# Attention scores from plain f32 matmuls on two halves of the array, in place of split operands

## The chip, the cores and the metric

The kernel runs on one core of a Trainium2 chip. The metric is the device time in microseconds (us) of one execution; where several runs are shown, their median. The profile is one execution recorded by the hardware profiler.

## The reference, cut to what matters

```python
# q, k, v: (4, 8, 1152, 64)    w_in: (512, 2048)    w_out: (2048, 512), all f32
q_pool = q.reshape(B, H, S // 2, 2, D).mean(axis=3)             # 576 queries a head
scores = (1 / sqrt(D)) * q_pool @ k^T                           # 576 x 1152 a head
scores = scores - max(scores, axis=-1)
attn   = exp(scores) / (sum(exp(scores)) + 1e-9)
x      = attn @ v                                               # heads joined: 2304 x 512
h      = x @ w_in                                               # 2304 x 2048
out    = (h * clip(h + 3, 0, 6) / 6) @ w_out                    # 2304 x 512
```

## The kernel before

The 32 heads are taken as 16 pairs (`NG`). The 576 queries of a head are cut into 64 and four times 128. A pair thus has nine score tiles of 128 query rows: one that holds the 64 rows of both heads (`j` is None in the code), and four for each head. There are 144 tiles `i` in all. A tile's 1152 keys are taken in three pieces `c` of 384 columns.

**Operands of the scores.** The kernel wants more precision than one f32r matmul gives, so it splits each operand into an upper part (rounded to f32r) and the remainder. For each head, `upper_k` and `lower_k` put both parts of k beside each other (64 + 64 columns); `turn_k` (L333) transposes this on TensorE into 128 rows, `take_k` copies it from PSUM to SBUF (`kT`). `pool_q` writes the sum of neighbouring queries twice beside each other, `turn_q` (L346) transposes it, and `take_q` splits the result into `qh` (ScalarE, L355) and `ql` (VectorE, L357). One piece of scores (`scores`, L384) is then two f32r matmuls with a contraction of 128: `qh` with both parts of k, and `ql` with both parts of k. A None tile takes four, two for each head, with zeros in the rows of the other head.

**What follows a score piece.** `least` (L392, VectorE) copies it out of PSUM with the running minimum of the negated scores; `expo` (ScalarE), `recip` (VectorE) and `normal` (GpSimd) make the softmax; `turn` (L423) transposes it on TensorE in three pieces of three 128x128 transposes, in f32; `take` copies these out; `values` (L448) multiplies with v in plain f32, each head into 64 of the 128 output rows (64 columns of the array). The result is split and spilled to DRAM, two groups of query columns a pair (320 and 256).

**The rest.** The weights of the gated layer are converted to a split form early and stored in DRAM (`w_d`). `layer` (L172) and `project` (L205) read them back, 512 KB at a time, for 6 chunks of 256 tokens times 16 blocks of the hidden dimension. The last 768 tokens are done at the end, when the attention is over.

**Order.** The order of the instructions on every engine and on the DMA queue (all DMAs are issued by SyncE) is written out in advance by `Order.run`, a list planner with a cost for each step and a place in a priority list; the chip then keeps that order on each engine. Tiles below `WIDE` use the first part's PSUM layout: score buffers `v`, two of two banks each, evacuated two pieces at once and then one. At tile `WIDE` the function `second_part` takes these banks away; from then on the scores have two banks `s`, and `layer` and `project` get theirs and run between the attention's steps.

The matmuls of the scores:

```python
            for x in q_t[g % 2]:
                for jj in ((0, 1) if j is None else (j,)):
                    o = 0 if j is None else 2 * REST + t * P
                    ops.append((x[:, jj, o:o + P], kT[g, jj, c]))
            for m, (x, kk) in enumerate(ops):
                nc.tensor.matmul(ps, x, kk.rearrange("p t k -> p (t k)"), start=(m == 0), stop=(m == len(ops) - 1))
```

Of the kernel before, what the change touches and what calls it, by code (L numbers as in the profile page):

```python
# [11 lines left out]
F32 = mybir.dt.float32  # L12
# [12 lines left out]
NEAR = 5  # L25
WIDE = 40
# [87 lines left out]
def pooled_attention_then_gated_mlp(ctx, tc, q, k, v, w_in, w_out, out):  # L114
# [130 lines left out]
    with ExitStack() as a:  # L245
        ld = a.enter_context(tc.tile_pool(name="ld", bufs=2))
        kq = a.enter_context(tc.tile_pool(name="kq", bufs=4 * KT // KC))
        sp = a.enter_context(tc.tile_pool(name="sp", bufs=5))
        sm = a.enter_context(tc.tile_pool(name="sm", bufs=6))
# [9 lines left out]
        for n in range(2):  # L259
            both = []  # L260
            for nm in ("qh", "ql"):
                t = const.tile([P, 2, QW], F32R, name=f"{nm}{n}")
                for j in range(2):
                    z = slice(REST * (1 - j), REST * (2 - j))
                    nc.vector.tensor_copy(out=t[:, j, z], in_=zero.to_broadcast([P, REST]))
                both.append(t)
            q_t.append(both)
# [4 lines left out]
        EARLY = [(0, 0), (0, 1), (None, 0), (1, 0), (1, 1)] + TILES[5:]  # L272
        NTI = len(TILES)
        GROUPS = ((0, REST + 2 * P), (REST + 2 * P, SQ - REST - 2 * P))

        def tiles(g):
            return TILES if g else EARLY

# [8 lines left out]
        def load_k(eng, g, j):  # L287
            b, h = pair(g, j)
            kr_t[g, j] = ld.tile([P, KT, D], F32, tag="kr", name="kr")
            nc.sync.dma_start(out=kr_t[g, j], in_=k[b, h].rearrange("(p t) d -> p t d", p=P))  # L290

        def load_q(eng, g, j):
            b, h = pair(g, j)
            qr_t[g, j] = ld.tile([QP, QT, 2, D], F32, tag="qr", name="qr")
            nc.sync.dma_start(out=qr_t[g, j], in_=q[b, h].rearrange("(p t r) d -> p t r d", p=QP, r=2))
# [14 lines left out]
        def pool_q(eng, g, j, r):  # L310
            if r == 0:
                qp_t[g, j] = ld.tile([QP, QT, 2, D], F32, tag="qp", name="qp")
            x = qr_t[g, j]
            by[eng].tensor_tensor(out=qp_t[g, j][:, :, r, :], in0=x[:, :, 0, :], in1=x[:, :, 1, :], op=ALU.add)

        def upper_k(eng, g, j):
            ks_t[g, j] = ld.tile([P, KT, 2, D], F32R, tag="ks", name="ks", bufs=1)
            copy(eng, ks_t[g, j][:, :, 0, :], kr_t[g, j])

        def lower_k(eng, g, j):  # L320
            ks = ks_t[g, j]
            by[eng].tensor_tensor(
                out=ks[:, :, 1, :], in0=kr_t[g, j], in1=ks[:, :, 0, :].bitcast(F32), op=ALU.subtract
            )
# [4 lines left out]
        def turn_k(eng, g, j, c):  # L329
            ps = tr_t["k", g, j, c] = near(g)[0].tile([P, KC, P], F32R, tag=near(g)[1], name="ptk")  # L330
            for t in range(KC):
                src = ks_t[g, j][:, KC * c + t, :, :].rearrange("p r d -> p (r d)")
                nc.tensor.transpose(ps[:, t, :], src, identr)  # L333

        def take_k(eng, g, j, c):
            kT[g, j, c] = kq.tile([P, KC, P], F32R, tag="kT", name="kT")
            copy(eng, kT[g, j, c], tr_t.pop(("k", g, j, c)))


        QPARTS = (((0, REST, 0), (REST, SQ // 2, 2 * REST)), ((0, SQ // 2, REST + SQ // 2),))  # L340

        def turn_q(eng, g, j, half):
            ps = tr_t["q", g, j, half] = near(g)[0].tile([P, SQ // 2], F32, tag=near(g)[1], name="ptq")
            for t in range(QT // 2):
                src = qp_t[g, j][:, half * (QT // 2) + t, :, :].rearrange("p r d -> p (r d)")
                nc.tensor.transpose(ps[:, t * QP:(t + 1) * QP], src, ident[:QP, :QP])  # L346

        def take_q(eng, g, j, half):
            qh, ql = q_t[g % 2]
            ps = tr_t["q", g, j, half]  # L350
            for c0, c1, to in QPARTS[half]:
                to = to or REST * j
                o = slice(to, to + c1 - c0)
                if eng == "ACT":
                    nc.scalar.copy(out=qh[:, j, o], in_=ps[:, c0:c1])  # L355
                else:
                    nc.vector.tensor_tensor(  # L357
                        out=ql[:, j, o], in0=ps[:, c0:c1], in1=qh[:, j, o].bitcast(F32), op=ALU.subtract
                    )

        def pieces(i):

            return [(0, 2), (2, 3)] if i < WIDE else [(c, c + 1) for c in C3]

        def bank(i):
            return "v" if i < WIDE else "s"

        def scores(eng, i, c):
            g, n = divmod(i, NTI)
            j, t = tiles(g)[n]  # L370
            tag = bank(i)
            if c in [c0 for c0, _ in pieces(i)]:
                pool, n = (ps_m["s"], 1) if tag == "s" else (ps_w, 2)
                ps_t[i] = pool.tile([P, n, DM], F32, tag=tag, name="pqk", bufs=2), c
                ps_t[i, c] = ps_t[i]
            tile, c0 = ps_t[i]
            ps = tile[:, c - c0, 0:NK]
            ops = []
            for x in q_t[g % 2]:
                for jj in ((0, 1) if j is None else (j,)):  # L380
                    o = 0 if j is None else 2 * REST + t * P
                    ops.append((x[:, jj, o:o + P], kT[g, jj, c]))
            for m, (x, kk) in enumerate(ops):
                nc.tensor.matmul(ps, x, kk.rearrange("p t k -> p (t k)"), start=(m == 0), stop=(m == len(ops) - 1))  # L384

        def least(eng, i, c):
            if c == 0:
                s_t[i] = sp.tile([P, S], F32, tag="s", name="s")
                cm_t[i] = sm.tile([P, KC], F32, tag="cm", name="cm")
            s, cm = s_t[i], cm_t[i]  # L390
            end = dict(pieces(i))[c]
            nc.vector.tensor_scalar(  # L392
                out=s[:, c * NK:end * NK].rearrange("p (c k) -> p c k", k=NK), in0=ps_t.pop((i, c))[0][:, 0:end - c, 0:NK],
                scalar1=-SCALE, scalar2=cm[:, c - 1:c] if c else None,
                op0=ALU.mult, op1=ALU.min, accum_out=cm[:, end - 1:end],
            )
# [32 lines left out]
        def take(eng, i, c):  # L429
            g, gr = group(i)  # L430
            j, t = tiles(g)[i % NTI]
# [132 lines left out]
        room = dict(kr=2, qr=2, qp=2, ks=1, vr=2, tr=2, kT=12, tx=1, s=2, S=5, pt0=1, pt1=1, av=1, xo=2,  # L564
# [5 lines left out]
        def halves(j, t):  # L570

            if j is None:
                return [(0, 0), (1, 0)]
            return [(j, n) for n in range(2) if t in ((0, 1), (1, 2, 3))[n]]

        for g in range(NG):
            z0 = 3 * NTI * g
            lead = z0 - 3 * NTI
            early = g == 0
            for j in range(2):  # L580
                add(("lk", g, j), lead - 8 + 9 * j, {"SP": (470, 2500, 900)}, partial(load_k, g=g, j=j), (), ("kr",))
                add(("lq", g, j), lead - 8 + 9 * j + .5, {"SP": (470, 2500, 900)}, partial(load_q, g=g, j=j), (), ("qr",))
                z = lead + 2 + 7 * j
                for r in range(2):
                    cost = {"DVE": (480, 560)} if early else {"POOL": (1100, 1110)}
                    add(("pq", g, j, r), z + 1 + r, cost, partial(pool_q, g=g, j=j, r=r),
                        [("pq", g, j, 0)] if r else [("lq", g, j)], () if r else ("qp",), ("qr",) if r else ())
                cost = {"ACT": (580, 680)} if early else {"POOL": (780, 790), "ACT": (580, 680, 4)}
                add(("uk", g, j), z, cost, partial(upper_k, g=g, j=j), [("lk", g, j)], ("ks",))
                cost = {"DVE": (690, 760)} if early else {"POOL": (1490, 1500)}  # L590
                add(("dk", g, j), z + .5, cost, partial(lower_k, g=g, j=j), [("uk", g, j)], (), ("kr",))
                for c in C3:
                    add(("tk", g, j, c), z + 4 + 2 * c, {"PE": (255, 475)}, partial(turn_k, g=g, j=j, c=c),
                        [("dk", g, j)], (near(g)[1],), ("ks",) if c == 2 else ())
                    add(("ek", g, j, c), z + 4 + 2 * c, MOVE, partial(take_k, g=g, j=j, c=c),
                        [("tk", g, j, c)], ("kT",), (near(g)[1],))
                for n in range(2):
                    add(("tq", g, j, n), z + 5 + 2 * n, {"PE": (255, 475)}, partial(turn_q, g=g, j=j, half=n),
                        [("pq", g, j, 1)], (near(g)[1],), ("qp",) if n else ())
                    needs = [("tq", g, j, n)]  # L600
                    if g > 1:
                        needs += [("mm", NTI * (g - 1) - x, 2) for x in (1, 2)]
# [160 lines left out]
```

## Time and profile before

| what | value |
|---|---|
| median of 3 runs | 989.78 us (989.46 to 992.21) |
| span of the profiled execution | 988.8 us |
| TensorE (PE) busy | 942.5 us, 95% |
| VectorE (DVE) busy | 590.6 us, 60% |
| ScalarE (ACT) busy | 532.6 us, 54% |
| GpSimd (POOL) busy | 362.2 us, 37% |
| DMA | 204 MB, 206 GB/s over the span |

PE busy counts a matmul from its start to its modelled end, and matmuls overlap in the array; so the distance between the starts of two matmuls, and not the duration of one, says what a matmul costs the engine. PEld is the loading of the stationary operand, which overlaps matmuls.

### The profile page before, as it was taken

Reading aid. Unit: us, or ns where it says so; the run is one execution under the profiler, and the core shown is the slowest. Engines: PE = TensorE matmul, PEld = TensorE weight load, DVE = VectorE, ACT = ScalarE, POOL = GpSimd, SP = SyncE. Lnnn points to the kernel's source line nnn. Section 1 sums busy time; section 2 is a strip of 40 time slices with the busy share of each in tenths; the row PEclk is TensorE's granted clock in tenths of the full one; section 3 lists DMA queues with packets and bytes.
Section 4 is the critical chain, followed back from the end, with each engine's and each line's share of the span. In section 5 each row is a group of like instructions: output and inputs, shape, how many; then the busy total and the mean of one; then the engine's idle time right before and its main releaser. Section 6 shows DMA issues by size and latency. Waiting matters only on the chain.

```text
span 988.8 us, 17816 instructions
## 1 busy us (share of the span) xinstructions
PE 942.5 (95%) x6288; PEld 783.6 (79%) x6288; DVE 590.6 (60%) x1752; ACT 532.6 (54%) x1098; POOL 362.2 (37%) x338
## 2 busy tenths in 40 slices
PE   5898997999999999999999999999999999999997
PEld 4676676677678888888888878888898887788886
DVE  5787788678687766566575756566565552222222
ACT  4786786666565656455564555455564542222222
POOL 3876867545565434333251423323121110000000
PEclk9999997999999999999999999999999999999999
DMA  5875565788777476568475766557565668633332
GB/s 174 274 231 192 178 202 174 227 288 287 265 252 240 153 224 199 183 207 285 159 252 163 235 223 217 200 176 276 185 226 168 223 229 283 219 127 126 127 124 85
DMA packets 80888, 204.06 MB, mean 206 GB/s; under 512 B 7840, under 2 KB 31392, under 8 KB 80800
## 3 DMA queue, kind: packets, MB, share of 16 engines
q1 hardware_dynamic: 80800, 202.93, 62.6%
q8 instruction: 50, 0.82, 0.3%
q14 instruction: 38, 0.31, 0.1%
HBM read 171.97 MB, written 30.93 MB: 205 GB/s over the span
## 4 chain that ended last, share of the span: by engine, by line
PE 80%; DVE 9%; DMA 5%; ACT 3%; issue 2%; POOL 1%; SPq 0%; ACTq 0%; DVEq 0%; POOLq 0%
PE ph L172 18%; PE po L205 15%; PE pav L448 14%; PE pqk L384 13%; PE ptp L423 11%; PE pt L205 4%; DVE s L392 3%; DMA w<-w_d 3%; PE ptk L333 2%; PE ptq L346 1%; DVE gl L190 1%; DMA raw<-in_moe_w_in_dram 1%; DMA raw<-in_moe_w_out_dram 1%; ACT s L401 1%; DVE pcv L503 1%
## 5 line engine op out<-in xcount | busy, mean ns | idle before, releaser
L412 POOL TENSOR_SCALAR s<-s,den 128x1152 f32<-128x1152 f32 x144 | 177.8, 1235 | 340.1 <-DVE den L408 204.9
L423 PE MATMUL ptp<-ident,s 128*128 128x128 f32 x1296 | 209.1, 277 | 8.3 <-ACT pt L306 4.8
L401 ACT ACTIVATE s<-s,cm 128x1152 f32<-128x1152 f32 x144 | 181.7, 1262 | 40.7 <-DVE s L392 39.6
L384 PE MATMUL pqk<-kT,qh 128*128 128x384 f32 x480 | 184.9, 402 | 6.3 <-DVE s L392 5.2
L172 PE MATMUL ph<-mxmxh,w 128*128 128x256 f32 x896 | 184.3, 289 | 6.0 <-DMA w<-w_d 4.9
L423 PEld LDWEIGHTS ptp<-ident,s 128*128 128x128 f32 x1296 | 156.6, 142 | 39.2 <-issue 9.6
L306 ACT COPY pt<-ptp 128x384 f32<-128x384 f32 x296 | 138.7, 481 | 77.3 <-PE ptp L423 75.0
L392 DVE TENSOR_SCALAR_CACHE_REDUCE s<-pqk,cm 128x384 f32<-128x384 f32 x248 | 151.0, 609 | 32.0 <-PE pqk L384 27.7
L384 PE MATMUL pqk<-kT,ql 128*128 128x384 f32 x480 | 156.8, 343 | 0.0
L172 PEld LDWEIGHTS ph<-mxmxh,w 128*128 128x128 f32 x896 | 147.1, 191 | 11.5 <-DMA w<-w_d 4.5
L448 PE MATMUL pav<-pt,vr 128*64 128x256 f32 (+1 forms) x1152 | 149.2, 410 | 0.1
L205 PE MATMUL po<-w,gh 128*128 128x512 f32 x448 | 140.6, 395 | 0.0
L177 ACT ACTIVATE r<-ph,three 128x256 f32<-128x256 f32 (+1 forms) x128 | 63.8, 499 | 142.2 <-PE ph L172 141.9
L172 PE MATMUL ph<-mxmxl,w 128*128 128x256 f32 x448 | 126.7, 283 | 0.0
L448 PEld LDWEIGHTS pav<-pt,vr 128*64 128x64 f32 x1152 | 78.9, 137 | 56.7 <-issue 6.2
L181 DVE SCALAR_TENSOR_TENSOR r<-r,ph 128x256 f32<-128x256 f32 (+1 forms) x128 | 57.6, 450 | 97.8 <-ACT r L177 97.2
L308 DVE COPY pt<-ptp 128x384 f32<-128x384 f32 x136 | 74.9, 553 | 56.3 <-PE ptp L423 55.8
L392 DVE TENSOR_SCALAR_CACHE_REDUCE s<-pqk 128x384 f32<-128x384 f32 (+1 forms) x144 | 95.4, 662 | 16.6 <-PE pqk L384 15.0
L384 PEld LDWEIGHTS pqk<-kT,qh 128*128 128x128 f32 x480 | 89.1, 193 | 16.1 <-DVE s L392 11.4
L205 PE MATMUL po<-w,gl 128*128 128x512 f32 x224 | 93.5, 417 | 6.8 <-DVE gl L190 3.5
L205 PEld LDWEIGHTS po<-w,gh 128*128 128x128 f32 x448 | 84.8, 189 | 14.8
L190 DVE TENSOR_TENSOR gl<-r,gh 128x256 fp32r<-128x256 f32 (+1 forms) x128 | 79.1, 618 | 28.7 <-ACT gh L185 28.2
(55 smaller groups left out, 1132.8 us busy)
## 6 DMA issues: line engine op xcount, KB each, us to landing
w<-w_d SPq DMA_DIRECT2D x224, 512.0 KB, 4.6
w_d<-scratch SPq DMA_DIRECT2D x32, 512.0 KB, 3.7
kr<-in_k_dram SPq DMA_DIRECT2D x32, 288.0 KB, 4.6
qr<-in_q_dram SPq DMA_DIRECT2D x32, 288.0 KB, 4.8
vr<-in_v_dram SPq DMA_DIRECT2D x16, 576.0 KB, 5.3
raw<-in_moe_w_in_dram SPq DMA_DIRECT2D x16, 512.0 KB, 4.3
raw<-in_moe_w_out_dram SPq DMA_DIRECT2D x16, 512.0 KB, 4.3
mxmxh<-xh_d SPq DMA_DIRECT2D x7, 512.0 KB, 6.1
```

The costliest lines, as they stand in the source:

```text
L172: nc.tensor.matmul(ps, w[:, wi, cs], x[:, c, :], start=(m == 0), stop=(m == 3 * NCC - 1))
L177: nc.scalar.activation(out=r6, in_=ps, func=AF.Relu, bias=three)
L190: nc.vector.tensor_tensor(out=gl, in0=r6, in1=gh.bitcast(F32), op=ALU.subtract)
L205: nc.tensor.matmul(o, g[:, ts], w[:, wi, :], start=(f == 0 and n == 0), stop=(f == NFC - 1 and n == 2))
L306: nc.scalar.copy(out=out, in_=in_)
L308: by[eng].tensor_copy(out=out, in_=in_)
L384: nc.tensor.matmul(ps, x, kk.rearrange("p t k -> p (t k)"), start=(m == 0), stop=(m == len(ops) - 1))
L392: nc.vector.tensor_scalar(out=s[:, c * NK:end * NK].rearrange("p (c k) -> p c k", k=NK), in0=ps_t.pop((i, c))[0][:, 0:end - c, 0:NK], scal ...
L401: nc.scalar.activation(out=s, in_=s, func=AF.Exp, bias=cm_t.pop(i)[:, KC - 1:], scale=-1.0, accum_out=den_t[i])
L412: nc.gpsimd.tensor_scalar(out=s, in0=s, scalar1=den_t.pop(i), scalar2=1.0, op0=ALU.mult, op1=ALU.mult)
L423: nc.tensor.transpose(ps[:, x, :], s_t[i][:, o:o + P], ident)
L448: nc.tensor.matmul(av[j * D:(j + 1) * D, :], vr_t[g][:, j, t, :], pt_t[g, gr][:, t, j, :], start=(t == 0), stop=(t == KT - 1),)
```

## The change

Scores are computed in plain f32. Neither k nor q is split.

- k of both heads of a pair is loaded in one DMA of 576 KB (before, two of 288 KB), and so is q. `join_k` puts the two heads beside each other (64 + 64 columns), `pool_q` does the same for q; so one transposition serves both heads: per pair 9 of k (f32 in place of 18 in f32r) and 6 of q (in place of 12).
- After it, rows 0 to 63 of `kT` and of q hold head 0 and rows 64 to 127 head 1. One step of `scores` issues two f32 matmuls with a contraction of 64: head 0 on rows 0 to 63 of the array, head 1 on rows 64 to 127, each into a PSUM bank of its own. The None tile is one f32 matmul with a contraction of 128 (the zeros are kept).
- Two tiles (the same rows of both heads) thus get their scores together, and take both `s` banks at once in the second part. `least` evacuates one piece of 384 at a time throughout.
- The pair's first tile needs both heads; the order `EARLY` of the first pair (head 0 first) is gone. `WIDE` is 41. `kT` has 6 buffers in place of 12, `s` in SBUF 7 in place of 5, the raw q one of double size in place of two. Loads of weights (`lw`) must keep their order.

```diff
-            both = []
-            for nm in ("qh", "ql"):
-                t = const.tile([P, 2, QW], F32R, name=f"{nm}{n}")
...
+            t = const.tile([P, QW], F32, name=f"q{n}")
+            nc.vector.tensor_copy(out=t[:, 0:2 * REST], in_=zero.to_broadcast([P, 2 * REST]))
...
+        def join_k(eng, g, j):
+            if j == 0:
+                ks_t[g] = ld.tile([P, KT, 2, D], F32, tag="ks", name="ks", bufs=1)
+            copy(eng, ks_t[g][:, :, j, :], kr_t[g][:, j])
...
-                nc.tensor.transpose(ps[:, t, :], src, identr)
...
+                nc.tensor.transpose(ps[:, t, :], ks_t[g][:, KC * c + t, :, :].rearrange("p j d -> p (j d)"), ident)
...
+        def take_q(eng, g, half):
+            t, ps = q_t[g % 2], tr_t["q", g, half]
+            if half == 0:
+                for j in range(2):
+                    d = slice(j * D, (j + 1) * D)
+                    copy(eng, t[d, j * REST:(j + 1) * REST], ps[d, 0:REST])
+                copy(eng, t[:, 2 * REST:REST + SQ // 2], ps[:, REST:])
+            else:
+                copy(eng, t[:, REST + SQ // 2:], ps)
...
+        def space(i):
+
+            if i < WIDE:
+                t = ps_w.tile([P, 2, DM], F32, tag="v", name="pqk", bufs=2)
+                return [t[:, x, 0:NK] for x in range(2)]
+            return [ps_m["s"].tile([P, DM], F32, tag="s", name="pqk")[:, 0:NK] for _ in range(2 if i % NTI else 1)]
...
+            if j is None:
+                if i >= WIDE or c != 1:
+                    ps_t[i] = space(i)
+                ps_t[i, c] = ps_t[i].pop(0)
+                nc.tensor.matmul(ps_t[i, c], q_t[g % 2][:, 0:P], kk, start=True, stop=True)
+            else:
+                o = 2 * REST + t * P
+                for x, ps in enumerate(space(i)):
+                    ps_t[i + x, c] = ps
+                    d = slice(x * D, (x + 1) * D)
+                    nc.tensor.matmul(ps, q_t[g % 2][d, o:o + P], kk[d, :], start=True, stop=True)
...
             nc.vector.tensor_scalar(
-                out=s[:, c * NK:end * NK].rearrange("p (c k) -> p c k", k=NK), in0=ps_t.pop((i, c))[0][:, 0:end - c, 0:NK],
...
+                out=s[:, c * NK:(c + 1) * NK], in0=ps_t.pop((i, c)), scalar1=-SCALE,
...
-                    add(("mm", i, c), z + c, {"PE": (350 * len(heads), 350 * len(heads) + 220)},
...
+                        add(("mm", i, c), z + c, {"PE": (680, 880)}, partial(scores, i=i, c=c),
```

## Rows read from the trace of the kernel before

**Rows 1.** The page: TensorE's busy time, and the chain that ended last by engine.

```profile
PE 942.5 (95%) x6288; PEld 783.6 (79%) x6288; DVE 590.6 (60%) x1752; ACT 532.6 (54%) x1098; POOL 362.2 (37%) x338
...
PE 80%; DVE 9%; DMA 5%; ACT 3%; issue 2%; POOL 1%; SPq 0%; ACTq 0%; DVEq 0%; POOLq 0%
PE ph L172 18%; PE po L205 15%; PE pav L448 14%; PE pqk L384 13%; PE ptp L423 11%; PE pt L205 4%; DVE s L392 3%; DMA w<-w_d 3%; PE ptk L333 2%; PE ptq L346 1%; DVE gl L190 1%; DMA raw<-in_moe_w_in_dram 1%; DMA raw<-in_moe_w_out_dram 1%; ACT s L401 1%; DVE pcv L503 1%
```

**Rows 2.** Windows of the whole core: busy us of each engine, granted clock (PEclk), DMA.

```profile
0.00:150.00 150.00, 129.58 (x868) 99.38 (x869) 110.18 (x319) 109.88 (x229) 104.34 (x108) 1.00 0.65 208
150.00:300.00 150.00, 137.98 (x934) 108.74 (x934) 114.34 (x331) 92.42 (x192) 85.71 (x82) 0.97 0.75 248
300.00:840.00 540.00, 533.94 (x3778) 455.57 (x3777) 325.64 (x1032) 291.12 (x608) 172.15 (x150) 1.00 0.65 214
840.00:988.80 148.80, 141.03 (x713) 119.95 (x712) 40.41 (x73) 39.15 (x72) 0.00 (x0) 0.98 0.42 136
```

**Rows 3.** Groups of TensorE matmuls by form: count, busy us, mean ns of one.

```profile
L384 PE MATMUL pqk<-kT,qh 128*128 128x384 f32 x480 | 184.9, 402 | 6.3 <-DVE s L392 5.2
...
L384 PE MATMUL pqk<-kT,ql 128*128 128x384 f32 x480 | 156.8, 343 | 0.0
...
L448 PE MATMUL pav<-pt,vr 128*64 128x320 f32 x576 | 82.4, 436 | 0.0
...
L333 PE MATMUL ptk<-identr,ks 128*128 128x128 f32 x288 | 39.1, 247 | 8.2 <-DVE ks L322 5.3 <-ACT kT L306 2.1 <-DVE ql L357 0.7
...
L346 PE MATMUL ptq<-ident,qp 96*128 96x96 f32 x192 | 28.0, 256 | 4.9 <-DVE kT L308 1.7 <-DVE ql L357 1.2 <-ACT kT L306 1.2
```

**Rows 4.** Timeline of TensorE matmuls: start us, us to the last end, instructions.

```profile
410.38 0.42 PE L384 MATMUL pqk<-kT,qh 128*128 128x384 f32 x1
...
410.82 0.49 PE L423 MATMUL ptp<-ident,s 128*128 128x128 f32 x3
411.06 0.42 PE L384 MATMUL pqk<-kT,qh 128*128 128x384 f32 x1
```

**Rows 5.** Timeline: an entry of `values` (L448), and the exit from it.

```profile
261.61 0.27 PE L423 MATMUL ptp<-ident,s 128*128 128x128 f32 x1
261.81 1.03 PE L448 MATMUL pav<-pt,vr 128*64 128x320 f32 x6
...
266.17 0.71 PE L448 MATMUL pav<-pt,vr 128*64 128x320 f32 x4
266.81 0.45 PE L384 MATMUL pqk<-kT,qh 128*128 128x384 f32 x1
267.09 0.34 PE L384 MATMUL pqk<-kT,ql 128*128 128x384 f32 x1
```

**Rows 6.** Timeline: transposes of k and of q, three each, and what follows.

```profile
337.93 0.37 PE L333 MATMUL ptk<-identr,ks 128*128 128x128 f32 x3
338.14 0.52 PE L423 MATMUL ptp<-ident,s 128*128 128x128 f32 x3
...
347.76 0.41 PE L346 MATMUL ptq<-ident,qp 96*128 96x96 f32 x3
348.01 0.49 PE L423 MATMUL ptp<-ident,s 128*128 128x128 f32 x3
```

**Rows 7.** Groups by form: evacuations of scores on VectorE.

```profile
L392 DVE TENSOR_SCALAR_CACHE_REDUCE s<-pqk,cm 128x384 f32<-128x384 f32 x248 | 151.0, 609 | 32.0 <-PE pqk L384 27.7
...
L392 DVE DVE_READ_ACCUMULATOR s<-pqk,cm 128x1 f32 x248 | 20.3, 82 | 0.0
...
L392 DVE TENSOR_SCALAR_CACHE_REDUCE s<-pqk 128x768 f32<-128x768 f32 x40 | 38.0, 950 | 5.3 <-PE pqk L384 5.2
```

**Rows 8.** Windows for the PSUM tile `ptq` alone: busy us of PE, PEld, DVE, ACT.

```profile
0.00:150.00 150.00, 10.47 (x66) 7.56 (x66) 9.67 (x30) 8.61 (x30) 1.00 0.65 208
```

**Rows 9.** The same for the PSUM tile `ptk`.

```profile
0.00:150.00 150.00, 13.14 (x87) 10.37 (x87) 4.42 (x8) 10.10 (x21) 1.00 0.65 208
```

**Rows 10.** DMA issues: count, KB each, median us from issue to landing.

```profile
kr<-in_k_dram SPq DMA_DIRECT2D x32, 288.0 KB, 4.6
...
vr<-in_v_dram SPq DMA_DIRECT2D x16, 576.0 KB, 5.3
```

More of the change, by code (lines that the diff above doesn't have):

```diff
@@ L376, in scores @@
[L376 to L384, printed above, removed]
+            j, t = TILES[n]
@@ L568, in pooled_attention_then_gated_mlp, with key @@
         MOVE = {"ACT": (400, 480), "DVE": (480, 555, 1.5)}
[L570 to L574, printed above, removed]
+        def key(i, c):
+            n = i % NTI
+            return "mm", i - (n and 1 - n % 2), c
         for g in range(NG):
@@ L583, in pooled_attention_then_gated_mlp @@
[L583 to L589, printed above, removed]
@@ L606, in pooled_attention_then_gated_mlp @@
[L606 to L607 removed]
+                cost = {"DVE": (480, 560)} if early else {"POOL": (1100, 1110)}
+                add(("pq", g, j), z + 1 + j, cost, partial(pool_q, g=g, j=j), [("pq", g, 0)] if j else [("lq", g)],
+                    () if j else ("qp",), ("qr",) if j else ())
+                cost = {("ACT", "POOL")[j]: (680, 760)} if early else {"POOL": (780, 790), "ACT": (580, 680, 4)}
@@ new lines, in pooled_attention_then_gated_mlp @@
+            for n in range(2):
+                add(("tq", g, n), z + 5 + 2 * n, {"PE": (255, 475)}, partial(turn_q, g=g, half=n),
+                    [("pq", g, 1)] + ([("mm", NTI * (g - 1) - 2, 2)] if g > 1 else []), (near(g)[1],), ("qp",) if n else ())
+                cost = 330 if n else 650
+                add(("eq", g, n), z + 5 + 2 * n, {"ACT": (cost, cost + 80), "DVE": (cost + 80, cost + 160, 1.5)},
+                    partial(take_q, g=g, half=n), [("tq", g, n)], (), (near(g)[1],))
@@ L608, in pooled_attention_then_gated_mlp @@
+            add(("lv", g), lead + 14, {"SP": (470, 2500, 1750)}, partial(load_v, g=g),
+                [key(NTI * g - 6 if g else 0, 0)], ("vr",))
+            for n, (j, t) in enumerate(TILES):
                 i = g * NTI + n
                 z = 3 * i
-                heads = (0, 1) if j is None else (j,)
                 gr = group(i)[1]
-                ends = dict(pieces(i))
+                pairs = j is not None
                 for c in C3:
-                    add(("mm", i, c), z + c, {"PE": (350 * len(heads), 350 * len(heads) + 220)},
-                        partial(scores, i=i, c=c),
-                        ([("mm", i, c - 1)] if c else [("mm", i - 1, 2)] if i else [])
-                        + ([("second",)] if i == WIDE and not c else [])
-                        + [("ek", g, jj, c) for jj in heads] + [("el", g, jj, h) for jj, h in halves(j, t)],
-                        (bank(i),) if c in ends else (), ("kT",) * (2 * (n == NTI - 1)))
-                    if c in ends:
-                        size = 420 * (ends[c] - c)
-                        add(("cp", i, ends[c] - 1), z + ends[c] - 1, {"DVE": (size + 140, size + 220)}, partial(least, i=i, c=c),
-                            [("mm", i, x) for x in range(c, ends[c])] + ([("cp", i, c - 1)] if c else []),
-                            () if c else ("S",), (bank(i),))
-                    add(("tp", i, c), z + TRN + c, {"PE": (330, 550)}, partial(turn, i=i, c=c),
@@ new lines, in pooled_attention_then_gated_mlp @@
+                    if key(i, c)[1] == i:
+                        prev = [("mm", i, c - 1)] if c else [key(i - 1, 2)] if i else []
+                        takes = ("s", "s") if pairs else ("s",)
+                        if i < WIDE:
+                            takes = () if not pairs and c == 1 else ("v",)
+                        add(("mm", i, c), z + c, {"PE": (680, 880)}, partial(scores, i=i, c=c),
+                            prev + ([("second",)] if i in (WIDE, WIDE + 1) and not c else [])
+                            + [("ek", g, c)] + [("eq", g, h) for h in range(2) if not c and (h == 0 or t)],
+                            takes, ("kT",) * (n == NTI - 2))
@@ new lines, in pooled_attention_then_gated_mlp @@
+                    frees = ("s",)
+                    if i < WIDE:
+                        frees = ("v",) if (j == 1 if pairs else c) else ()
+                    add(("cp", i, c), z + c, {"DVE": (540, 620)}, partial(least, i=i, c=c),
+                        [key(i, c)] + ([("cp", i, c - 1)] if c else []) + ([("cp", i - 1, c)] if j == 1 and i < WIDE else []),
+                        () if c else ("S",), frees)
+                    add(("tp", i, c), z + TRN + c, {"PE": (350, 570)}, partial(turn, i=i, c=c),
```

134 lines of the change are left out of this document (43 added, 91 removed).

## The prediction

> **What bounds the kernel now.** I read the page first. TensorE is busy 95% of the span, and it holds 80% of the chain that ended last [rows 1]. Such a busy share may hide idle stretches, so I cut the span into stages [rows 2]. From 300 to 840 us TensorE is busy 533.9 of 540 us, while VectorE has 325.6 and ScalarE 291.1: whatever TensorE spends more or less there is time, nearly one for one. The first 150 us are another matter: TensorE has 20.4 us idle and VectorE and ScalarE are both at 110. From 150 to 300 us TensorE has 12.0 us idle. The last 149 us hold no attention, and the change doesn't touch them. The granted clock is 1.00 or close to it in all stages, the 2.4 GHz level.
>
> So the question is what the change does to TensorE's issue time, from one matmul's start to the next one's.
>
> **Score matmuls.** From one score pair (410.38) to the next (411.06) pass 0.68 us, for two f32r matmuls and three transposes [rows 4]. One transpose takes 0.27 us from start to end [rows 5] and three end after 0.49 [rows 4], so they start 0.11 apart, 0.33 for three. That leaves 0.35 us for one head's piece of 384 columns, 0.70 for both heads. After the change, the same piece is two f32 matmuls. The trace has one kind of plain f32 matmul that isn't a transpose: `values`, with 320 columns [rows 3]. Its 576 records are 16 pairs x 18 matmuls x 2, so each f32 matmul is two records. Six records take 1.03 us; the last is 0.44 long, so three steps begin within 0.59, the first 0.32 and the next 0.27; four records in 0.71 confirm 0.27 a step [rows 5]. In each step two records run, one for each head, on different columns of the array. A step of 0.27 us at 2.4 GHz is two clocks a column; two steps hold one f32 matmul for both heads together. For 384 columns a step is 0.27 x 384/320 = 0.32 us, and a piece for both heads 0.65, if two row halves run beside each other as the two column halves do. That saves 0.05 us a piece, 192 times (16 pairs x 4 tile pairs x 3), and as much on each of the 48 pieces of None tiles, since four f32r matmuls (0.70) become one f32 matmul (0.65).
>
> **Transposes.** Three of k take 0.21 us from start to the next instruction's start, three of q 0.25 [rows 6]. A pair now has 18 of k and 12 of q (288 and 192 over 16 pairs) [rows 3]: 6 x 0.21 + 4 x 0.25 = 2.26 us. After it, 9 of k in f32 with the size and type of the softmax's transposes, 3 x 0.33, and 6 of q, 2 x 0.25: 1.49. That saves 0.77 us a pair.
>
> **What the row halves cost on entry and exit.** Before and after `values` TensorE stops, though nothing is waited for [rows 5]. The last transpose starts at 261.61 and the first of `values` at 261.81, 0.20 in place of 0.11: 0.09 us lost on entry. The first step then takes 0.32 in place of 0.27: 0.05 for a load of 64 stationary columns that was not done ahead. On exit two steps of 0.27 from 266.17 end at 266.71, and the scores start at 266.81: 0.10 lost; the next matmul follows 0.28 later, where 0.18 is usual: 0.10 for 128 stationary columns. The transposes of q, which use 96 of the 128 rows but all of the columns, show no such gap on either side: their 0.25 for three is less than the softmax's 0.33 [rows 6]. So it's the division of the array that costs, not a shorter contraction. The Trainium skill says so for both kinds of division (TensorEngine Tiling (Array Packing), Key Properties): a change of the tiling mode, as against a change of tile, drains the engine; 64 rows by 128 columns is one of its modes. The trace agrees for column tiles; no run shown here has row tiles.
>
> Today's kernel enters such a mode at least 32 times, for two groups of `values` in each of 16 pairs. After the change it does for each of the 192 paired pieces, between transposes and gated-layer matmuls that use the whole array. I price entry at 0.09 + 0.10 (128 columns in each half, loaded side by side as the column halves are) and exit at 0.10 + 0.08 (between 0.05 and 0.10, as the load before a short transpose may hide part of it): 0.37 us a piece. The bounds are 0 (row halves may need no change of mode) and 0.39, plus 0.10 if the loads of the two halves follow one another. I take 0.37, since `values` is the nearest row, and a division of the array like this one.
>
> **Sum for the second part.** `WIDE` = 41 leaves 46 tile pairs, 138 pieces, all of them alone: a piece takes both `s` banks, and the next can't start before VectorE has emptied them, 2 x (0.61 + 0.08) us [rows 7], in which the planner puts other matmuls. 138 x 0.37 = +51. Against it 138 x 0.05 = 7, 33 None pieces x 0.05 = 1.7, and transposes for 11 pairs x 0.77 = 8.5: -17. Net +34 us, on an engine that is full.
>
> **Sum for the first part.** 54 pieces x 0.37 = 20; some follow each other with two `v` buffers, I take one in six, so 17. Savings: 54 x 0.05 + 12 x 0.05 + 5 x 0.77 = 7. TensorE +10. Of this, part falls into its 20.4 us of idle time, and the other engines get relief: the q copies (9.7 on VectorE, 8.6 on ScalarE [rows 8]) shrink to about a third, since the split is gone and one copy serves two heads; those of k (4.4 and 10.1 [rows 9]) to half; together some 19 us. But `least` now makes three evacuations of 0.69 for a tile where one of 1.03 and one of 0.69 did [rows 7]: +0.35 x about 35 tiles, 12 us. Net relief 7 us over two engines with 220 us of work: 3 to 4 each. The start waits for both heads: a 576 KB load lands 0.7 us after a 288 KB one would [rows 10], with two joins in series in place of one upper part and one remainder: +1. I take +5 for the first part; the ends are -3 (all of TensorE's extra lies in idle time) and +11.
>
> **What costs nothing.** GpSimd loses the remainder of k and half of the sums' count, and at 37% nothing waits for its throughput [rows 1]. DMA bytes stay the same, with half as many issues for k and q. The raw q has one buffer: a load of q that waits for `pool_q` would hold up the weight loads behind it on SyncE's queue, and `layer` behind those. GpSimd is idle two thirds of the second part [rows 2], so `pool_q` is early; without that cover, each pair would cost TensorE up to the 4.6 us that a load of 288 KB takes to land [rows 10]. The order among `lw` is the order in which they are used already.
>
> Total: +34 + 5 = +39 on a span of 988.8, 1027.8. The median of the runs stands 1.0 above that span; I say **1028 us**.
>
> **The rivals.** (a) *Row halves need no change of mode.* For it speaks that contraction and columns are different directions of the array. The gain is then all of the savings: -17 in the second part, and -7, -4 of relief and +1 in the first: -27, **962 us**. The Trainium skill's TensorE page (TensorE: Matmul & The Clock Gate, Part 3) has a span model of this kind, in which tiles in different row groups start a few ns apart and entering them has no price. Its measurements are of tiles alone, not between full matmuls, and `values` shows that the price is at the border. (b) *Only the stop remains.* If the stationary operands are loaded ahead, a piece costs 0.19: 138 x 0.19 = 26 less 17 is +9, and the first part about 0: **998**. It decides for slower from about 0.12 us a piece, where the second part's 17 us are used up. (c) *The halves don't run beside each other.* Two banks and twice the results in each step may be too much for the way out to PSUM; `values` writes each partition from one head only. A piece is then four steps, 1.29 in place of 0.70: 192 x 0.59 = 113, less 12 for transposes, about **1090**, and up to 1150 with the mode's price. (d) *PSUM.* The halves empty both `s` banks one after the other, 1.4 us before the next piece can start. In the second part 138 pieces come within some 650 us, one every 4.7 us, and VectorE is 60% busy [rows 2], so this should fit; if it cost 0.3 us on each piece, it would add 40 to any other case.
>
> **How the numbers follow.** Mode price in full: 0.55, with 1012 to 1046 as its own range (0.28 to 0.49 us a piece, first part from -3 to +11). (a) 0.22, 955 to 972. (b) 0.12, 985 to 1008. (c) and (d) together 0.11, above 1046. To leave out no more than 2 in 10, the range has to reach to both signs: 958 to 1050. A change under 0.3%, 3 us, can't be told from none. Faster is (a) and a little of (b): 0.24. Same: 0.04, from (b). Slower: 0.72.
>
> **What would show it.** In the changed trace, the start of a paired score matmul should stand 0.20 us after the last transpose, the two heads' records within 10 ns of each other, the second step 0.42 later (0.32 and 0.10 of loading), and what follows 0.10 late. From 300 us on, TensorE should still be full, with the attention some 35 us longer and the last 149 us unchanged. The transposes of k should count 144 and of q 96. The prediction is wrong if paired scores start 0.11 us after a transpose (then (a)), if the two heads' records start 0.3 us or more apart (c), or if TensorE waits for `least` in the second part (d).

## The result: slower by 1.4%, where 3.9% was predicted

| | before | after |
|---|---|---|
| median | 991.0 us | 1004.8 us (1003.3 to 1009.5) |
| ratio, 95% interval | | 1.0141 (1.0107 to 1.0174) |
| span of the profiled execution | 988.8 us | 1007.7 us |

The direction is the one predicted and the time lies in the range, but the loss is 14 us and not 38. The mean granted clock of TensorE (1.00 is the 2.4 GHz level) goes with the time: the four executions of the changed kernel run from 1003.3 us at 0.997 to 1009.5 at 0.989. A straight line through the executions of each kernel here, with one slope for all, gives some 8 us for 0.01 of the clock, an estimate that is used below where a few us matter. The page of the changed kernel, TensorE's busy time and the chain that ended last:

```profile
PE 969.0 (96%) x5952; PEld 678.6 (67%) x5952; DVE 549.9 (55%) x1713; ACT 506.1 (50%) x1025; POOL 292.6 (29%) x284
...
PE 86%; DMA 5%; DVE 5%; ACT 2%; issue 1%; POOL 1%; SPq 0%; POOLq 0%; DVEq 0%; ACTq 0%
```

Against [rows 1], TensorE is 26 us busier with 336 fewer instructions, and its share of the chain has gone from 80 to 86% while VectorE's has fallen from 9 to 5. The windows of the changed kernel, with the columns of [rows 2]:

```profile
0.00:150.00 150.00, 128.09 (x750) 70.01 (x750) 101.37 (x331) 94.79 (x189) 86.62 (x95) 0.98 0.67 214
150.00:300.00 150.00, 142.31 (x868) 90.47 (x867) 107.36 (x325) 87.47 (x176) 74.54 (x75) 0.95 0.75 244
300.00:840.00 540.00, 538.36 (x3488) 382.38 (x3487) 295.62 (x974) 279.03 (x576) 131.44 (x115) 1.00 0.62 201
```

From 300 us on TensorE's idle time has gone from 6.1 to 1.6 us. VectorE, ScalarE and GpSimd have less to do in each of these stages. The groups of the matmuls that changed, with the columns of [rows 3]:

```profile
L364 PE MATMUL pqk<-kT,q 64*128 64x384 f32 x768 | 185.2, 549 | 6.5 <-DVE s L371 6.4
...
L358 PE MATMUL pqk<-kT,q 128*128 128x384 f32 x96 | 41.5, 523 | 0.6 <-ACT kT L297 0.6
...
L318 PE MATMUL ptk<-ident,ks 128*128 128x128 f32 x144 | 26.1, 293 | 10.5 <-POOL ks L299 6.5 <-ACT kT L297 2.5 <-ACT q L297 1.0
...
L328 PE MATMUL ptq<-ident,qp 96*128 96x96 f32 x96 | 15.0, 267 | 3.3 <-ACT q L297 2.7 <-ACT kT L297 0.6
```

192 pieces of two heads with two records each are the 768; 48 None pieces are the 96. Transposes of k and q are down to 144 and 96. One paired piece in the timeline of the changed kernel (start, us to the last end), between a transpose and the gated layer, from three narrow windows:

```profile
467.68 0.27 PE L401 MATMUL ptp<-ident,s 128*128 128x128 f32 x1
467.88 0.59 PE L364 MATMUL pqk<-kT,q 64*128 64x384 f32 x2
...
467.88 0.92 PE L364 MATMUL pqk<-kT,q 64*128 64x384 f32 x4
468.73 0.38 PE L172 MATMUL ph<-mxmxh,w 128*128 128x256 f32 x1
468.95 0.28 PE L172 MATMUL ph<-mxmxl,w 128*128 128x256 f32 x1
```

The entry takes 0.20 us in place of 0.11. The two heads' first records, about 0.59 us each, both end within 0.59: they run beside each other. The last two take 0.48 and end 0.92 after the start, so they start at 0.44 less a few ns; the raw starts are 467.880 and 468.306, a first step of 0.43 where a bare one is 0.32. The second step is 0.42 (to 468.73), and the next matmul's start comes 0.22 later, where 0.12 is usual in the gated layer (where a transpose follows, its successor starts 0.17 later in place of 0.11). So: 0.09 on entry, 0.10 for loading, 0.10 on exit, 0.10 for the next load (0.06 if a transpose follows, as in most cases). This is a price of about 0.36 a piece, which the prediction put at 0.37.

**Where the missing 24 us are.** I split TensorE's time from starts alone: for each pair of neighbouring instructions the 20th percentile of the distance between their starts, over all pairs with the same shapes and modes in the traces compared, is called issue time, and whatever a distance has beyond it is called waiting. The instruction ahead of the pair has to be told apart too, since in the kernel before a score matmul behind transposes starts 0.03 us after the last of them and its own successor 0.25 later, in place of 0.11 and 0.18. The three stretches are up to the 97th matmul of `layer`, from there to the first matmul of the last 512 tokens, and the rest. Each kernel's profiled execution, us (for e11 and e12 below, whose scores have other steps, with percentiles of their own):

```
                          issue time               waiting
before                    200 + 568 + 130 = 897    53 + 26 + 1 = 80
changed                   205 + 597 + 130 = 932    46 + 16 + 1 = 63
changed, run again        205 + 597 + 130 = 932    42 + 18 + 1 = 60
```

TensorE's own issue time rose by 35 us, 5 and 29 in the first two stretches (predicted: 44, +10 and +34). Its waiting fell by 17 to 20, and this is what the prediction didn't have beyond 5 us. The two figures are estimates: with other percentiles, and with pairs told apart more finely, the rise comes out between 30 and 43 us and the fall between 12 and 27. The method moves time from one to the other and leaves their difference, the longer span, as it is. Waiting also holds the stretches at the 1.2 GHz level, in which a transpose follows another after 0.21 us in place of 0.11: of the 80, 63 and 60 us some 8, 11 and 5. The kernel before doesn't show this waiting as idle time, because a matmul's modelled end reaches far into its successor. One such wait in the timeline of the kernel before, for the gated layer's remainder on VectorE:

```profile
413.51 0.28 PE L172 MATMUL ph<-mxmxh,w 128*128 128x256 f32 x1
414.01 0.50 PE L205 MATMUL po<-w,gl 128*128 128x512 f32 x1 [0.22 <-DVE gl L190]
```

The step from the first to the second is 0.50 us where 0.12 is usual: 0.38 of waiting, of which the profile counts 0.22 as idle.

### The profile page after: what moved, and what is told of

It reads as the page before. It is cut to its first block, busy times and chain, and to the rows that moved or that the text cites. A ratio compares the mean times of both kernels' runs of the same rounds, so it can differ in the third digit from the quotient of the medians.

```text
span 1007.7 us, 16771 instructions
## 1 busy us (share of the span) xinstructions
PE 969.0 (96%) x5952; PEld 678.6 (67%) x5952; DVE 549.9 (55%) x1713; ACT 506.1 (50%) x1025; POOL 292.6 (29%) x284
## 4 chain that ended last, share of the span: by engine, by line
PE 86%; DMA 5%; DVE 5%; ACT 2%; issue 1%; POOL 1%; SPq 0%; POOLq 0%; DVEq 0%; ACTq 0%
PE ph L172 19%; PE po L205 15%; PE pqk L364 14%; PE pav L426 14%; PE ptp L401 14%; PE pt L205 4%; PE pqk L358 3%; DVE s L371 2%; DMA w<-w_d 2%; PE ptk L318 1%; DMA raw<-in_moe_w_in_dram 1%; PE ptq L328 1%; DMA raw<-in_moe_w_out_dram 1%; DVE pcv L481 1%; DMA qr<-in_q_dram 1%
## 5 line engine op out<-in xcount | busy, mean ns | idle before, releaser
L401 PEld LDWEIGHTS ptp<-ident,s 128*128 128x128 f32 x1296 | 146.3, 142 | 110.0 <-issue 47.5
L401 PE MATMUL ptp<-ident,s 128*128 128x128 f32 x1296 | 203.9, 282 | 8.6 <-POOL s L390 3.8
L371 DVE TENSOR_SCALAR_CACHE_REDUCE s<-pqk,cm 128x384 f32<-128x384 f32 x288 | 169.8, 613 | 56.6 <-PE pqk L364 42.5
L364 PE MATMUL pqk<-kT,q 64*128 64x384 f32 x768 | 185.2, 549 | 6.5 <-DVE s L371 6.4
L297 ACT COPY pt<-ptp 128x384 f32<-128x384 f32 x289 | 133.2, 480 | 115.8 <-PE ptp L401 112.8
L299 DVE COPY pt<-ptp 128x384 f32<-128x384 f32 x143 | 78.3, 554 | 53.5 <-PE ptp L401 52.7
L364 PEld LDWEIGHTS pqk<-kT,q 64*128 64x128 f32 x768 | 61.8, 189 | 50.3 <-issue 24.4
L371 DVE TENSOR_SCALAR_CACHE_REDUCE s<-pqk 128x384 f32<-128x384 f32 x144 | 77.8, 552 | 29.2 <-PE pqk L364 18.4
L172 PEld LDWEIGHTS ph<-mxmxl,w 128*128 128x128 f32 x448 | 85.4, 191 | 1.4
L185 ACT CAST gh<-r 128x256 fp32r<-128x256 f32 (+1 forms) x128 | 55.4, 432 | 54.6 <-DVE r L181 53.7
```

The lines of the kernel that those rows point to most:

```text
L172: nc.tensor.matmul(ps, w[:, wi, cs], x[:, c, :], start=(m == 0), stop=(m == 3 * NCC - 1))
L297: nc.scalar.copy(out=out, in_=in_)
L299: by[eng].tensor_copy(out=out, in_=in_)
L364: nc.tensor.matmul(ps, q_t[g % 2][d, o:o + P], kk[d, :], start=True, stop=True)
L371: nc.vector.tensor_scalar(out=s[:, c * NK:(c + 1) * NK], in0=ps_t.pop((i, c)), scalar1=-SCALE, scalar2=cm[:, c - 1:c] if c else None, op0= ...
L401: nc.tensor.transpose(ps[:, x, :], s_t[i][:, o:o + P], ident)
```

## The experiments

Theory A: TensorE's waits are a cushion; when it gets slower, the other engines catch up and part of the added time disappears. Theory B: the waits went because the split's work left VectorE and ScalarE. Theory C: the mode price counts for less than 0.36 us a piece. Ratios are to the kernel before on the same chip, with their 95% intervals.

**e1: the price of the modes, taken away.** Edit to the changed kernel (operands in f32r):

```diff
-                    d = slice(x * D, (x + 1) * D)
-                    nc.tensor.matmul(ps, q_t[g % 2][d, o:o + P], kk[d, :], start=True, stop=True)
+                    for m in range(2):
+                        nc.tensor.matmul(ps, q_t[g % 2][:, o:o + P], kk, start=(m == 0), stop=(m == 1))
```

> The changed kernel, with each paired piece made by four f32r matmuls over all 128 rows (two into each bank) in place of two f32 ones on the halves. It leaves out the separation of the heads and the lower bits of the operands. TensorE then never changes its mode for scores: 192 pieces cost 0.70 us in place of 0.65 + 0.37, 61 us less issue time. Theory A (TensorE has waits that fill up when it gets slower and come back when it gets faster): about 965 us, ratio 0.97 to 0.98. Theory B (the waits went because the split's work left VectorE and ScalarE): they stay away here, about 944 us, ratio 0.95 to 0.96. Theory C (the mode costs far less of the time than 0.37 us a piece, since much of it falls into waits): above 985 us, ratio above 0.99.

Measured: 967.9 us, ratio 0.9748 (0.9712 to 0.9785). Issue time 876, waiting 82. C is out: without the modes the changed kernel is 37 us shorter. So is B as the only cause: the split's work is still gone, and the waits are back. Its windows, with the columns of [rows 2]:

```profile
0.00:150.00 150.00, 124.76 (x767) 90.87 (x767) 104.17 (x342) 97.85 (x194) 88.81 (x98) 0.98 0.68 219
150.00:300.00 150.00, 136.29 (x897) 106.42 (x896) 109.99 (x335) 89.81 (x182) 77.71 (x78) 0.98 0.78 256
300.00:840.00 540.00, 535.99 (x3669) 450.81 (x3669) 295.42 (x976) 282.52 (x589) 125.94 (x110) 1.00 0.66 218
```

TensorE's idle time there is 25.2, 13.7 and 4.0 us, where the changed kernel has 21.9, 7.7 and 1.6.

**e2 and e5: the relief alone.** Edits to the kernel before; e2 has the first hunk, e5 both (in both, q's tiles are also filled with zeros at the start, which adds 7 us on GpSimd):

```diff
-                to = to or REST * j
+                to, c1 = to or REST * j, c0 + 8
...
-                else:
+                elif False:
                     nc.vector.tensor_tensor(
                         out=ql[:, j, o], in0=ps[:, c0:c1], in1=qh[:, j, o].bitcast(F32), op=ALU.subtract
```

> The kernel before, with every copy of the split q (ScalarE's upper part and VectorE's remainder) cut to 8 columns, the rest of q left at zero: most scores are zero, the order of every engine is kept, TensorE has the same matmuls. VectorE loses about 25 us of work and ScalarE 20. Theory A: little, 985 to 991 us, ratio 0.993 to 1.0. Theory B (relief of VectorE and ScalarE is what took TensorE's waits away): 966 to 975 us, ratio 0.975 to 0.984. Theory C says nothing of it.

> The kernel before without the remainder of q (its copies are left out, that operand stays zero) and with the upper part's copies cut to 8 columns; TensorE's matmuls and every order are kept. VectorE loses 33 us of work and ScalarE about 13. Theory A (TensorE's waits fill up when it gets slower; relief of the others counts for little): 983 to 987 us, ratio 0.991 to 0.995. Theory B (the relief took the waits away): 972 us or less, ratio 0.98 or less.

Measured: e2 986.4 us, ratio 0.9948 (0.9929 to 0.9967); e5 985.7, 0.9941 (0.9912 to 0.997). The copies have a cost that doesn't depend on their columns: in e2 VectorE lost only 16 us and ScalarE 13, in e5 24 and 13. Relief gives about 5 us at most: the mean granted clock of e2's and e5's executions was 0.993 and 0.994, that of the kernel before beside them 0.990, which by the estimate above is 2 to 3 of the 5 us. B is a small part.

**e3 and e8: more issue time alone.** Edit to the kernel before (e8; e3 has `j == 0` alone):

```diff
-            for m, (x, kk) in enumerate(ops):
+            for m, (x, kk) in enumerate(ops := [ops[0]] * 2 * (j == 0 and c > 0 and t + c < 5) + ops):
```

> The kernel before, with the first matmul of each score piece of head 0 issued three times (its product counts threefold): 192 pieces x 0.35 us = 67 us more issue time on TensorE and nothing else. Theory A: part of it falls into waits, 1030 to 1042 us, ratio 1.04 to 1.05. Theory B and C: nearly all of it shows, 1052 to 1058 us, ratio 1.062 to 1.068.

> The kernel before with the first matmul issued three times in 112 of the score pieces of head 0 (its product counts threefold): 39 us more issue time on TensorE, which is what the change adds net, and nothing else. Theory A, with two thirds of it showing as with 67 us: 1016 to 1020 us, ratio 1.025 to 1.029. Theory A with the first microseconds absorbed more than the last: 1008 to 1014, ratio 1.017 to 1.023. Theory B: 1028 to 1031, ratio 1.037 to 1.04.

Measured: e3 1037.9 us, ratio 1.0453 (1.0419 to 1.0488): of 66 us of issue time 46 show. e8 1018.1, 1.0252 (1.021 to 1.0293): of 39 us 27 show. Both as A says. The windows of e3, in which nothing but matmuls was added:

```profile
0.00:150.00 150.00, 135.76 (x928) 109.50 (x929) 105.82 (x303) 105.39 (x220) 99.06 (x102) 0.99 0.61 200
150.00:300.00 150.00, 140.95 (x956) 115.95 (x955) 110.50 (x319) 91.38 (x184) 83.62 (x79) 0.97 0.72 235
300.00:840.00 540.00, 536.61 (x3774) 467.21 (x3773) 323.03 (x1013) 282.68 (x588) 176.49 (x154) 1.00 0.60 198
```

Idle time in the first 150 us goes from 20.4 [rows 2] to 14.2 and in the next 150 from 12.0 to 9.1; from 300 to 840 it goes from 6.1 to 3.4. Waiting by starts: 61 in place of 80; in e8 it is 63, as in the changed kernel.

**e4, e6 and e10: work added on VectorE.** e4 and e6 in the changed kernel, e10 in the kernel before; one such addition behind each copy (e4: 1152 columns, 32 of them; e6 and e10: 288 columns, 80 of them):

```diff
+nc.vector.tensor_tensor(out=idle, in0=idle, in1=idle, op=ALU.add)
```

> The changed kernel with 32 additions of 1152 columns on VectorE, one behind each copy of q, whose result nobody reads: about 43 us more on VectorE, as much as the change took from it. Theory A: TensorE is slow enough to hide it, up to 4 us more than the changed kernel, ratio 1.014 to 1.018. Theory B: the waits return, 1020 to 1030 us, ratio 1.03 to 1.04. Theory C says nothing of it.

> The changed kernel with 80 additions of 288 columns on VectorE, one behind each copy of q and of k, whose result nobody reads: about 35 us more on VectorE, in pieces as short as the split's own. Theory A, with the cost of the 32 long additions due to their length (each holds up the score evacuation queued behind it): 1005 to 1013 us, ratio 1.014 to 1.022. Theory B, by which VectorE's load counts however it is cut: 1022 to 1030 us, ratio 1.032 to 1.04.

> The kernel before with 80 additions of 288 columns on VectorE, spread over the copies of k and q, whose result nobody reads: 35 us more on VectorE, as was put into the changed kernel. If a written order can't use relief but passes delays on (work added where nobody planned it costs, work taken away gains little, in either kernel), it costs as much here as there: 1006 to 1012 us, ratio 1.015 to 1.021. If only the changed kernel is sensitive, or if VectorE has room here: up to 996, ratio up to 1.005.

Measured: e4 1032.7 us, ratio 1.0398 (1.0352 to 1.0443); e6 1022.9, 1.0292 (1.024 to 1.0344); e10 1009.2, 1.0187 (1.0156 to 1.0218). The additions were longer than I reckoned: 49 us in e4 (1656 and 1412 ns each), 51 in e6 and 56 in e10 (687 to 705 ns each). Against their own kernels they cost 28, 18 and 19 us by medians; e4 and e6 come to 25 and 15 by the ratios to the kernel before. Taken alone, e4 spoke for B. e10 shows what it is: the same short additions as in e6 cost as much in the kernel before, where nothing had been relieved, so they say nothing of the relief. Work that the written order doesn't know of delays what stands behind it, about 0.3 to 0.35 us a microsecond when short and 0.5 to 0.57 when long; work taken away gives at most 0.15 to 0.2 (e2, e5: 5 us for 29 to 37).

**e9, e13, e15, e17: the account put together in the kernel before.** e9 and e15 are e8 with e5's edit. e13 also has:

```diff
-            copy(eng, kT[g, j, c], tr_t.pop(("k", g, j, c)))
+            copy(eng, kT[g, j, c][:, :, 0:P - 120 * j], tr_t.pop(("k", g, j, c))[:, :, 0:P - 120 * j])
```

and e17 is e8 with GpSimd's remainder of k cut to a ninth (`ks[:, 0, 1, :]` in place of `ks[:, :, 1, :]`).

> The kernel before with the 39 us more on TensorE of the 112 longer score pieces, and without the remainder of q and most of its upper part, together. If absorption and relief are the whole account, this lands where the changed kernel did: 1003 to 1013 us, ratio 1.012 to 1.022. If something else of the change (loads, buffers, two tiles at a time) also shortened the run, this stays above: ratio 1.025 or more.

> The kernel before with the 39 us more on TensorE, without the split of q, and with the copies of the second head's transposed k cut to 24 columns (its scores use the first head's k): the change's net issue time and nearly all of its relief, in the order of the kernel before. If issue time, absorption and relief are the whole account, 1.012 to 1.016, level with the changed kernel. If something else of the change shortens the run, 1.018 or more.

> The kernel before with the 39 us more on TensorE and without the split of q, again, beside the changed kernel on one chip: 1.016 to 1.022; within 0.3% of the changed kernel if the gap seen between them was chance, 0.4% or more above it if it was not.

> The kernel before with the 39 us more on TensorE, and GpSimd's remainder of k cut to one of its nine blocks (the transposes of a head all read that block): some 35 us less on GpSimd. If GpSimd's relief gives the last 10 us: 1004 to 1009 us, ratio 1.014 to 1.018. If not, as with the 39 us alone: ratio 1.021 to 1.029.

> The changed kernel itself, again, for a narrower interval beside the two others: 1.012 to 1.018.

Measured: e9 1.0194 (1.0151 to 1.0237); e15 1.024 (1.0207 to 1.0273), e13 1.0235 (1.0206 to 1.0264) and, beside them on one chip, the change again, e14, 1.0135 (1.0104 to 1.0166); e17 1.0234 (1.0207 to 1.0262). Once TensorE is slower, the relief of any engine makes no difference that these runs can tell: e8's 1.0252 stays. And the account doesn't close: the change is 10 us shorter than the kernel before with its issue time, and 8 to 9 us when the granted clocks are allowed for (0.9935 on average in e14, 0.9905 in e15, 0.992 in e13).

**e16 and e18: score buffers.** `bufs` of `sp` and room `S` at 5 (e16) and 6 (e18) in place of 7 in the changed kernel.

> The changed kernel with 5 score buffers in SBUF, as the kernel before has, in place of 7 (and 6 small ones in place of 8). If the last 10 us of the account come from the two more buffers, which the halved transposed k made room for: 1012 to 1020 us, ratio 1.02 to 1.028. If not: ratio 1.011 to 1.017.

> The changed kernel with 6 score buffers in place of 7. If the buffers count, between the two: ratio 1.015 to 1.022. If not, 1.011 to 1.017.

Measured: 1.0132 (1.0103 to 1.0161) and 1.017 (1.0142 to 1.0199). No trend with the number of buffers; the two more don't explain the 10 us.

**e7: the order.**

```diff
-{"PE": (680, 880)}
+{"PE": (1020, 1040) if pairs else (680, 880)}
```

> The changed kernel with the planner told 1020 in place of 680 ns for a paired piece, which is what its profile shows, so that the orders of all engines are made for the true price. If the remaining waits come from an order made for the wrong price, 990 to 1000 us, ratio 0.999 to 1.009; if they are the same waits as in the kernel before, 1000 to 1008, ratio 1.009 to 1.017.

Measured: 1.0153 (1.0117 to 1.0189). An order made for the true price is no better.

**e11 and e12: scores without modes.** Both pad q of each head with zeros in the other head's rows; e11 in f32r, which leaves out the lower bits of q and k, e12 in f32:

```diff
-                    nc.tensor.matmul(ps, q_t[g % 2][d, o:o + P], kk[d, :], start=True, stop=True)
+                    nc.tensor.matmul(ps, q_t[g % 2][:, x, o:o + P], kk, start=True, stop=True)
```

> The changed kernel with f32r operands and one f32r matmul per head and piece over all 128 rows, q of each head padded with zeros in the other head's rows. It keeps the heads apart but leaves out the lower bits of q and k. TensorE: 192 x 0.35 + 48 x 0.53 + 12 for transposes = 104 us less than the kernel before, and no change of mode for scores. Theory A (0.6 to 0.7 of it shows, as waits come back): 919 to 930 us, ratio 0.927 to 0.938. Nearly all of it: 887 to 897, ratio 0.895 to 0.905. Another engine takes over: above 945, ratio above 0.953.

> The changed kernel in f32 with q of each head padded with zeros in the other head's rows, so that each paired piece is two f32 matmuls one after the other over all 128 rows: 1.29 us and no change of mode, in place of 0.65 + 0.36. Per piece 0.28 us more, 54 us in all. Mode price 0.36 and 0.6 to 0.7 of it showing: 1037 to 1043 us, ratio 1.046 to 1.052. If the modes cost the run only half of that: 192 x 0.46 = 88 us more issue time, 1058 to 1067 us, ratio 1.067 to 1.077.

Measured: e12 1055.2 us, ratio 1.0651 (1.0619 to 1.0683), 50 us above the changed kernel. One of its pieces, in its timeline:

```profile
502.02 0.82 PE L401 MATMUL ptp<-ident,s 128*128 128x128 f32 x6
502.68 0.81 PE L358 MATMUL pqk<-kT,q 128*128 128x384 f32 x2
503.33 0.49 PE L401 MATMUL ptp<-ident,s 128*128 128x128 f32 x3
```

A plain f32 matmul over the whole array (this one is a None piece) enters after six transposes at 0.11, with nothing lost, and takes 0.65 to the next start. The paired pieces of e12 are two of these. By the issue time of its own trace, 990, it adds 58 us to the changed kernel's 932, and 50 show. My 54 was right within 4, but the share that shows is 0.87 and not 0.65, with waiting at 51 in place of 63. e11: 937.3 us, ratio 0.9458 (0.9421 to 0.9494), the shortest of all kernels here, for those who can do with f32r scores. TensorE's issue time falls by 102 us to 795, and half of it shows: waiting rises to 130. Part of that is the clock: TensorE was at the 1.2 GHz level for 34 us (17 in the kernel before) and its mean granted clock was 0.982 (0.991), so some 17 us of the 130 are steps at that level, where it is 8 of 80 before.

```profile
PE 863.7 (92%) x5520; PEld 679.8 (73%) x5520; DVE 544.8 (58%) x1713; ACT 513.4 (55%) x1055; POOL 295.4 (32%) x288
```

No other engine is near full there. That the rest is lost in chains between engines, which TensorE no longer covers, is argued and not shown.

## Why the prediction was right and wrong

**Right: what the array does.** The prediction had right the mode price (0.36 us against 0.37), that it is paid on entry and exit of row halves as of column halves, that the two halves run beside each other, the step of 0.32, the counts of transposes. 189 separate entries are in the trace for 192 pieces; I had counted 183. The Trainium skill's rule that a change of tiling mode drains the engine (TensorEngine Tiling (Array Packing), Key Properties) agrees with the trace, 0.09 us on entry and 0.10 on exit. The span model of the Trainium skill (TensorE: Matmul & The Clock Gate, Part 3) lets each further tile add about 4 ns and has no term for the border. Inside a piece the trace is close to it: the second half starts 7 ns after the first. Rival (a), no change of mode, (b), operands loaded ahead, and (c), halves one after the other, are excluded by the rows of the paired piece above: 0.20 us on entry, 0.10 of loading, records 7 ns apart. For (d), TensorE waits 6.4 us for `least` in the whole run, where it waited 5.2 [rows 3].

**Luck: that the time lies in the range.** The range of 958 to 1050 us was stretched over rivals of both signs. The case that the trace confirms, the mode price in full, had 1012 to 1046 as its own range (its bounds, added up, give 1008 to 1051), and 1004.8 lies below it. It lies where the prediction put rival (b), which the trace excludes.

**Wrong: the step from issue time to time.** The failing sentence is that from 300 us on "whatever TensorE spends more or less there is time, nearly one for one", because it is busy 533.9 of 540 us there. The second stretch, which begins some 40 us earlier and ends some 12 later, holds 26 us of waiting behind that busy share, of which 16 to 18 were left after the change. So the second part's +34 came out as +19 to +21 (594 us before, 613 and 615 after): issue time rose by 29 there, and 8 to 10 of it went into waits. In the first stretch I let 5 of 10 us pass to the run, and next to none did: 53 us of waiting became 42 to 46, and the stretch went from 253 us to 251 and 247, with 2.3 us of transposes moved behind it. With matmuls added to the kernel before, 0.69 of the added issue time shows, at 39 us as at 66; the same rate on the change's 35 us gives 24, where 14 (medians) to 19 (profiled runs) showed. I also priced the net issue time at 44 where the split into issue time and waiting gives 35. By single steps the terms hold: between transposes, a paired piece takes 1.00 us where the pieces of the two heads took 0.70, 0.30 more, and 192 of these less the savings on None pieces and transposes are some 42 us. So whether a term of the sum was mis-sized stays open; the percentiles may be what differs. A slip of count, 12 None pieces in the first part in place of 15, is worth 0.15 us.

**The relief** was reckoned for the first part only, as 3 to 4 us of work on each of two engines. Over the whole run VectorE has 41 us less to do and ScalarE 26. Taken away alone, 29 and 37 us of such work were worth 3 to 5 us of time (e2, e5); beside the slower TensorE, the worth was not measurable.

**What stays open.** The change is 10 us shorter than the kernel before with its issue time added by hand (1.0135 against 1.0252, 1.024, 1.0235). 3 to 4 us of this is issue time, since e8 has 936 against 932. The rest lies in the first stretch, which takes 247 to 251 us in the changed kernel and 256 to 259 in e8, e9, e13, e15 and e17; the second takes 612 to 614 in these and 613 to 615 in the changed kernel. Part of the rest is where the time was added: 84 of e8's 224 added matmuls, 15 of its 39 us, fall into the first stretch, where the change adds 5, and 21 of the softmax's transposes, 2.3 us, lie behind that stretch in the changed kernel and in it in e8. Copies of q and k, GpSimd's remainder, score buffers and the planner's price, each by itself, don't account for what is left; they were not taken away together. The order of the first pair, the evacuation in single pieces, and two tiles at a time were not tried apart, nor was it measured whether a wait that falls on a mode's gap costs only once. More score buffers in the kernel before were not tried.

## What to carry to other kernels

Dividing the array cost about 0.36 us each time it was entered and left between full matmuls, so the work inside has to save more than that. Here it held 0.65 us of work: enough against the same f32 products on the whole array (1.29 us; e12 is 50 us longer), too little against the split f32r products (0.70 us) of the kernel before. And an engine that is 99% busy is not yet one whose every microsecond counts. With matmuls, look at the distances between starts, and test the exchange rate by adding a known number of harmless matmuls before trusting a sum on that engine. In these kernels, whose order is written in advance, added work on VectorE cost at once, and relief gave back a fraction.

## What the runs showed of the hardware

Two f32 matmuls with 64 rows each, into two banks, start 7 ns apart and take no longer than one over 128 rows: a step of 0.32 us for 384 columns. The weights of both halves load side by side too, 0.10 us for both. The exchange rate of TensorE's issue time isn't constant: from 795 us (e11) to 897 (before) a microsecond shows as 0.5, from there to 963 (e3) as 0.7, and from 932 (changed) to 990 (e12) as 0.87. At one granted clock, by the estimate above, these would be nearer 0.6, 0.7 and 0.9 (0.982 in e11, 0.990 in the kernel before beside it, 0.994 in the changed kernel and 0.998 in e12).
